# Single-block expert layers with the rows stationary, a start with the scores first, the last exponentials reordered, scatters spread

## The chip, the cores and the metric

The kernel runs on one core of a Trainium2 chip. The metric is the device time of one execution in microseconds. A run here gives the median of several executions. All executions in this document are of the fast state; the granted clock of TensorE is given where it matters. The four batches of runs were timed on whatever chip they got, and the kernel before stood in each at 783.5, 796.53, 783.53 and 784.12 us. So only kernels of one batch are compared directly, or each with the kernel before of its own batch.

## The reference

```python
# attention: q, k, v (8, 8, 576, 64), s (8, 8, 576), all float32
scores = scale * np.matmul(q, k.transpose(0, 1, 3, 2))
cum = np.cumsum(np.maximum(s, 0.0), axis=-1)
bias = -(cum[:, :, :, None] - cum[:, :, None, :])
scores = np.where(causal, -1000000000.0, scores + np.minimum(bias, 0.0))
attn = softmax(scores);  x = attn @ v               # then heads side by side: (8, 576, 512)
# experts: 8 of them, w1 (8, 512, 1024), w2 (8, 1024, 512)
fresh_e = argmax(x[b, s] @ w_gate)
e = fresh_e if s == 0 or local_gate[b, s] < 0.5 else prev_e
h = np.maximum(x[b, s] @ w1[e], 0.0)
out[b, s] = p[e] * (h @ w2[e])                      # p = softmax of the gate's logits
```

(Shortened: softmax written as a word, loops left out.)

## The kernel before

Attention goes through 32 pairs of heads. The rows that come out are scattered into one list per expert in DRAM. Then the experts run in units: a "double" has two blocks of 128 rows, a "single" has one, and a "mixed" unit has two half blocks of two experts. For a unit, rows are gathered, transposed by VectorE (`xT`), go through the first layer (`layer1`, into `hT`) and the second (`layer2`), and the output rows are scattered. In `mm`, `lhsT` is the stationary operand and `rhs` the moving one. The trace shows each float32 multiplication as two records. "Tail" in the names is the last 64 of the 576 positions.

The start: idle multiplications (`spin(n)`, n products of the identity with itself, there to bring TensorE's clock up), the biases, and then the loop over pairs.

```python
    spin(18)
    nc.vector.tensor_scalar_max(s_sb, s_sb, 0.0)
    cum = t_in.tile([BH, S], F32, name="cum")
    nc.vector.tensor_tensor_scan(cum, ones, s_sb, 0.0, op0=Alu.mult, op1=Alu.add)
    # ... cut: rel = cum - cum[mid] for two groups, 3 + 6 transposes into one bank (bps) ...
    nc.vector.tensor_copy(bias, bps[:, :at])
    # ... cut ...
    tail_scores(0)
    for n in range(NPAIR + 1):
        load(n + 3)
        if n < NPAIR:
            for u, pieces in enumerate((((0, 0), (3, 1)), ((0, 1), (1, 1)), ((2, 0), (2, 1), (1, 0)))):
                scores(n, u)
                for piece in pieces:
                    weights(n, piece)            # exponentials, ScalarE
        # ... cut ...
        if n:
            rows(n - 1, 1); divide(n - 1, 1); rows(n - 1, 0)     # products with v, division
        else:
            spin(8)
        if n + 1 < NPAIR:
            tail_scores(n + 1)
        if n:
            divide(n - 1, 0)
        if n < NPAIR:
            gate_parts(n); beside_v(n)           # VectorE's transpose into v
```

The first layer. With two weights (mixed units) the rows are the stationary operand, with one they are the moving operand, 128 columns for a single and 256 for a double:

```python
        if len(w) > 1:
            # ... cut ...
                for c in range(DK):
                    for h in range(2):
                        d = slice(h * HALF, h * HALF + HALF)
                        mm(ps[d], lhsT=xT[i][:, c, d], rhs=w[h][:, c, f], start=(c == 0), stop=(c == DK - 1))
                nc.scalar.activation(hx[i][:, f], ps, Act.Relu)
            if last == FK:
                x = hx.pop(i).rearrange("p (f n) -> p f n", f=FK)
                for a in range(0, P, m):
                    for d in range(0, P, m):
                        nc.vector.transpose(hT[i][d : d + m, :, a : a + m], x[a : a + m, :, d : d + m])
            return
        per = 512 // n
        for g in range(first, last, per):
            ps = ps_h.tile([P, 512], F32, name="hp")
            for j in range(per):
                f = (g + j) * P
                y = ps[:, j * n : j * n + n]
                for c in range(DK):
                    mm(y, lhsT=w[0][:, c, f : f + P], rhs=xT[i][:, c, :], start=(c == 0), stop=(c == DK - 1))
```

Of the kernel before, what the change touches and what calls it, by code (L numbers as in the profile page):

```python
# [10 lines left out]
F32 = mybir.dt.float32  # L11
I32 = mybir.dt.int32
Act = mybir.ActivationFunctionType
# [5 lines left out]
P = 128  # L19
# [51 lines left out]
def kernel(  # L71
# [33 lines left out]
    with ExitStack() as main:  # L105
# [47 lines left out]
        for j in range(8):  # L153
# [7 lines left out]
        check = in_range(main.enter_context(tc.tile_pool(name="g_sb", bufs=1)), nc, recs, sort.total, sort.ones, out_of)  # L161
        hooks = [(2, last.choose), (2, last.codes), (6, last.rows), (6, last.fresh), (6, last.held), (8, last.share),
                 (11, last.hold), (11, last.hot), (13, last.count), (13, last.rank), (15, last.gates),
                 (16, lambda bank: [f(bank) for f in last.scatters]),
                 *((18 + 2 * i, lambda bank: next(tables, None)) for i in range(8)),
                 *((60 + 6 * i, lambda bank, f=f: f(bank)) for i, f in enumerate(check))]
        experts(tc, w1, w2, out, rows_d, ident, sort, early_units() + units(), hooks, x4, gx, ready)
    def number(x, most):
        return nc.values_load(x[0:1, 0:1], min_val=0, max_val=most, skip_runtime_bounds_check_because="a count")
# [44 lines left out]
def attention(ctx, tc, q, kz, vz, vx, s, w_gate, w_local, ident, lg, recs, keep, new_x, plan):  # L214
# [75 lines left out]
        for i in range(n):  # L290
            mm(banks[1][:, :P], lhsT=ident, rhs=ident, start=True, stop=True)  # L291

    spin(18)
    nc.vector.tensor_scalar_max(s_sb, s_sb, 0.0)
    cum = t_in.tile([BH, S], F32, name="cum")
    nc.vector.tensor_tensor_scan(cum, ones, s_sb, 0.0, op0=Alu.mult, op1=Alu.add)


    bps = ps_s.tile([P, 2, 512], F32, name="bps", tag="s")[:, 0]
    bias_of, at = {}, 0  # L300
    for g, (q0, q1) in enumerate(GROUPS):
        n = -(-q1 // P) * P if g == 0 else S
        rel = t_in.tile([BH, n], F32, name=f"rel{g}")
        nc.vector.tensor_scalar(rel, cum[:, :n], cum[:, MIDS[g] : MIDS[g] + 1], None, Alu.subtract)
        for c, a in enumerate(range(0, TS, P)):
            if a + P <= n:
                tr(bps[:, at : at + BH], rel[:, a : a + P], ident[:BH, :BH])
                bias_of[c, g] = at
                at += BH
    tail_bias = at  # L310
    for h in range(2):
        mm(bps[h * TL : h * TL + TL, at : at + NPAIR], lhsT=rel[:, TS:], rhs=ident[:BH, h:BH:2], start=True, stop=True)
    at += NPAIR
    bias = once.tile([P, at], F32, name="bias")
    nc.vector.tensor_copy(bias, bps[:, :at])
    at = bias_of[2, 0]
    nc.vector.memset(bias[TL:, at : at + BH], MASKED)
    tmp.close()
    p_sc = pool("p_sc", 2, reuse_waits="tile")

    def scores(n, u):

        qb, kb = ins[n][:2]
        ps = raw[u] = ps_s.tile([P, 2, 512], F32, name="ps", tag="s")
        scs[n, u] = p_sc.tile([P, 2, sum(z - a for _, _, a, z in UNITS[u])], F32, name=f"sc{u}")
        runs = []
        for c, g, a, z in UNITS[u]:
            if runs and runs[-1][0] == c and runs[-1][2] == a:
                runs[-1][2] = z
            else:  # L330
                runs.append([c, a, z, PIECE[c, g][1]])
        for c, a, z, at in runs:
            for h in range(2):
                d = slice(DH * h, DH * h + DH)
                mm(ps[:, h, at : at + z - a], lhsT=kb[d, c * P : c * P + P], rhs=qb[d, a:z],  # L335
                   start=True, stop=True)

    def weights(n, *pieces):

        for c, g in pieces:  # L340
            u, at, a, z = PIECE[c, g]
            for h in range(2):
                i = bias_of[c, g] + 2 * n + h
                nc.scalar.activation(scs[n, u][:, h, at : at + z - a], raw[u][:, h, at : at + z - a], Act.Exp,  # L344
                                     bias=bias[:, i : i + 1], scale=scale)
            if min(c * P + P, S) <= z and (c, g) in PIECE:
                at += c * P - a
                if at >= 0:
                    x = scs[n, u][:, :, at : at + P]
                    nc.gpsimd.affine_select(out=x, in_=x, compare_op=Alu.is_ge, fill=0.0, base=0,  # L350
                                            pattern=[[0, 2], [1, P]], channel_multiplier=-1)

    def tail_scores(n):
        for h in range(2):
            d = slice(DH * h, DH * h + DH)
            mm(scores_of_tail[d], lhsT=ins[n][1][:, TS:][:, d], rhs=ins[n][0][:, TS:], start=True, stop=True)  # L356

    def tail(n):

# [71 lines left out]
        t = ps_s.tile([P, 2, 512], F32, name="bank", tag="s")  # L431
        return [t[:, i] for i in range(n)]

    tail_scores(0)
    for n in range(NPAIR + 1):
        load(n + 3)
        if n < NPAIR:
            for u, pieces in enumerate((((0, 0), (3, 1)), ((0, 1), (1, 1)), ((2, 0), (2, 1), (1, 0)))):
                scores(n, u)
                for piece in pieces:  # L440
                    weights(n, piece)
                    if piece == (0, 0):
                        tail(n)
                for f in plan.pop((n, 3 + u), ()):
                    f(bank)
            seen_tail(n)
        for f in plan.pop((n, 0), ()):
            f(bank)
        if n:
            rows(n - 1, 1)  # L450
            divide(n - 1, 1)
            rows(n - 1, 0)
# [8 lines that stand above are left out]
            gate_parts(n)  # L461
            beside_v(n)
        if n and n % HP == 0:
            logits(n // HP - 1)
        for half in (1, 2):
            for f in plan.pop((n, half), ()):
                f(bank)
# [653 lines left out]
def experts(ctx, tc, w1, w2, out, rows_d, ident, sort, units, hooks=(), w3=None, gx=None, ready=None):  # L1121
# [86 lines left out]
    def layer1(i, first, last):  # L1208
# [4 lines left out]
        if first == 0:  # L1213
            hT[i] = fp.tile([P, FK * 2 * P], F32, name="hT")[:, : FK * n].rearrange("p (f n) -> p f n", f=FK)
        w = [ws[s][:, : DK * F].rearrange("p (c f) -> p c f", c=DK) for s in of[i]]
        if len(w) > 1:

            if first == 0:
                hx[i] = w3[:, WS : WS + F] if ready else fp.tile([P, F], F32, name="hx", bufs=1)
            for g in range(first, last, FK // 2):  # L1220
                ps = ps_h.tile([P, 512], F32, name="hp")
                f = slice(g * P, g * P + 512)
                for c in range(DK):
                    for h in range(2):
                        d = slice(h * HALF, h * HALF + HALF)
                        mm(ps[d], lhsT=xT[i][:, c, d], rhs=w[h][:, c, f], start=(c == 0), stop=(c == DK - 1))
                    tick()
                nc.scalar.activation(hx[i][:, f], ps, Act.Relu)  # L1228
            if last == FK:
                x = hx.pop(i).rearrange("p (f n) -> p f n", f=FK)  # L1230
                m = P // 4
# [4 lines that stand above are left out]
# [46 lines left out]
    if ready:  # L1282
# [4 lines left out]

        layer1(1, 0, FK)
        load(0)
        fetch(2)  # L1290
        fetch(3)
        for k in range(2):
            layer2(0, k)
        load(1)
        for k in range(2):
            turn_x(2, k)
# [71 lines left out]
```

## Time and profile before

| | before |
|---|---|
| median, range | 783.39 us, 782.95 to 784.17 |
| span of the profiled execution | 782.4 us |
| TensorE / VectorE / ScalarE / GpSimd busy | 99 / 43 / 30 / 23 % |
| TensorE's waits of 0.3 us and more | 1.6 at the start, 0.8 and 0.3 at the end of attention |
| pair 1's first score | 14.39 us |
| first expert multiplication | 241.87 us |
| start of the last run of multiplications | 755.09 us |

TensorE is full, so a change pays if it takes work off TensorE or closes one of these few gaps. The last three rows cut the span into pieces that can be compared one by one: the start up to 14.39, attention from there to 241.87 (227.48 us), the experts to 755.09 (513.22 us), and the rest (27.3 us). The lines themselves stand in the prediction below.

### The profile page before, as it was taken

To read this page: it belongs to the slowest core of one execution; us is meant where nothing else is said; L and a number is where in the kernel's file an instruction comes from. 1 tells how busy PE (TensorE), PEld (TensorE's weight loads), DVE (VectorE), ACT (ScalarE), POOL (GpSimd) and SP (SyncE) were. 2 spreads that over 40 slices of the span, in tenths; PEclk is the share of its full clock that TensorE was granted. 3 is DMA by queue.
4 is the path that set the end of the run, shared out by engine and by line. 5 is a ranking of instruction groups with operands and counts; after the bars stand their busy time and mean duration, and the time that the engine had idled before them with its cause. 6 is when DMAs were issued, how large, how long until landed. Compare 5 with 4: busy or idle time off the path is not lost.

```text
span 782.4 us, 17629 instructions
## 1 busy us (share of the span) xinstructions
PE 773.0 (99%) x6782; PEld 546.2 (70%) x6782; DVE 339.0 (43%) x1196; ACT 237.2 (30%) x611; POOL 176.2 (23%) x329
## 2 busy tenths in 40 slices
PE   9999999999999999999999999999999999999996
PEld 8888888888887846836677366773657736676762
DVE  2334444455566748315562156521565215635000
ACT  5777767776762111111111111111111111111110
POOL 4432345456450421011110111101111011011001
PEclk9999999999999999999999999999999999999999
DMA  9586679988655499966997569976699766994001
GB/s 314 187 300 194 201 244 327 326 285 262 210 208 217 131 354 390 409 228 221 376 395 297 199 224 380 392 290 208 233 365 389 297 211 228 368 409 175 10 13 44
DMA packets 64141, 205.56 MB, mean 263 GB/s; under 512 B 8269, under 2 KB 8301, under 8 KB 64048
## 3 DMA queue, kind: packets, MB, share of 16 engines
q1 hardware_dynamic: 55008, 173.55, 62.3%
q0 software_dynamic: 8896, 30.47, 10.4%
q8 instruction: 55, 0.90, 0.5%
q10 hardware_dynamic: 144, 0.33, 0.1%
q14 instruction: 38, 0.31, 0.1%
HBM read 181.08 MB, written 23.76 MB: 262 GB/s over the span
## 4 chain that ended last, share of the span: by engine, by line
issue 58%; PE 32%; POOL 5%; DVE 2%; POOLq 2%; DMA 1%; DVEq 0%
PE o L406 14%; PE ps L335 11%; POOL out_dram L1261 2%; POOL xg L1196 2%; PE hp L1243 2%; PE o L374 2%; PE o L291 1%; POOLq L1171 1%; DMA x_rows<-x,r_slot_i 1%; PE o L356 1%; PE bank L956 0%; DVE xT L1097 0%; POOL x_rows L1047 0%; PE bank L1107 0%; PE bank L981 0%
## 5 line engine op out<-in xcount | busy, mean ns | idle before, releaser
L1097 DVE STREAM_TRANSPOSE xT<-xg 32x128 f32<-32x128 f32 x576 | 174.1, 302 | 174.2 <-PE hp L1243 92.7
L1256 PE MATMUL yp<-w,hT 128*128 128x512 f32 (+1 forms) x528 | 216.4, 593 | 0.0
L1243 PE MATMUL hp<-xT,w 128*128 128x256 f32 (+1 forms) x1088 | 192.3, 337 | 0.3 <-DVE xT L1097 0.3
L1243 PEld LDWEIGHTS hp<-xT,w 128*128 128x128 f32 x1088 | 172.1, 191 | 24.6 <-issue 8.2
L344 ACT ACTIVATE sc<-ps,bias 128x256 f32<-128x256 f32 (+3 forms) x448 | 156.5, 482 | 53.6 <-PE ps L335 51.2
L1256 PEld LDWEIGHTS yp<-w,hT 128*128 128x128 f32 (+1 forms) x528 | 90.1, 180 | 114.6 <-issue 113.3
L1261 POOL DMA_INDIRECT out_dram<-y,at_gate x38 | 38.5, 1013 | 433.9 <-ACT y L1260 419.0
L406 PE MATMUL o<-v,sc 128*64 128x74 f32 x3072 | 113.6, 228 | 0.8 <-issue 0.8
L406 PEld LDWEIGHTS o<-v,sc 128*64 128x64 f32 x3072 | 108.8, 136 | 8.1 <-issue 4.3
L1247 ACT ACTIVATE hT<-hp 128x512 f32<-128x512 f32 x68 | 40.6, 597 | 193.0 <-PE hp L1243 193.0
L1260 ACT ACTIVATE y<-yp,at_gate 128x512 f32<-128x512 f32 x38 | 26.1, 687 | 239.8 <-PE yp L1256 233.6
L335 PE MATMUL ps<-q,k 64*128 64x320 f32 (+2 forms) x768 | 92.5, 386 | 0.1
L350 POOL TENSOR_SCALAR_AFFINE_SELECT sc<-sc 128x256 f32<-128x256 f32 x160 | 66.5, 420 | 115.9 <-issue 59.1
L335 PEld LDWEIGHTS ps<-q,k 64*128 64x128 f32 x768 | 68.9, 186 | 20.0 <-issue 4.8
L1256 PE MATMUL yp<-x,hT 128*128 128x512 f32 (+1 forms) x144 | 63.2, 594 | 0.0
L1234 DVE STREAM_TRANSPOSE hT<-x 32x256 f32<-32x256 f32 x64 | 27.9, 436 | 65.4 <-ACT x L1228 64.5
L1243 PEld LDWEIGHTS hp<-xT,x 128*128 128x128 f32 x320 | 46.1, 191 | 5.8 <-issue 2.6
L1243 PE MATMUL hp<-xT,x 128*128 128x128 f32 (+1 forms) x320 | 50.1, 317 | 0.0
L416 DVE RECIPROCAL recs<-o 128x4 f32<-128x4 f32 x64 | 12.1, 189 | 87.0 <-PE o L406 63.1
L1256 PEld LDWEIGHTS yp<-x,hT 128*128 128x128 f32 (+1 forms) x144 | 25.3, 178 | 26.2 <-issue 26.0
L1047 POOL DMA_INDIRECT x_rows<-x,r_slot_i x40 | 38.7, 968 | 10.1 <-issue 5.9
L419 DVE TENSOR_TENSOR x<-o,recs 128x292 f32<-128x292 f32 x64 | 34.4, 538 | 2.2
(162 smaller groups left out, 339.8 us busy)
## 6 DMA issues: line engine op xcount, KB each, us to landing
w<-in_w_dram SPq DMA_DIRECT2D x184, 512.0 KB, 9.5
x<-in_w_dram SPq DMA_DIRECT2D x56, 512.0 KB, 9.3
v<-in_vx_dram SPq DMA_DIRECT2D x32, 405.0 KB, 5.8
vt<-in_vz_dram SPq DMA_DIRECT2D x32, 320.0 KB, 3.9
k<-in_kz_dram SPq DMA_DIRECT2D x31, 320.0 KB, 5.1
q<-in_q_dram SPq DMA_DIRECT2D x32, 288.0 KB, 5.4
xg<-x_rows POOLq DMA_DIRECT2D x30, 293.0 KB, 8.5
x_rows<-r_empty SPq DMA_DIRECT2D x6, 293.0 KB, 3.6
```

Source lines behind the costliest of these rows:

```text
L335: mm(ps[:, h, at : at + z - a], lhsT=kb[d, c * P : c * P + P], rhs=qb[d, a:z], start=True, stop=True)
L344: nc.scalar.activation(scs[n, u][:, h, at : at + z - a], raw[u][:, h, at : at + z - a], Act.Exp, bias=bias[:, i : i + 1], scale=scale)
L350: nc.gpsimd.affine_select(out=x, in_=x, compare_op=Alu.is_ge, fill=0.0, base=0, pattern=[[0, 2], [1, P]], channel_multiplier=-1)
L406: mm(y, lhsT=w, rhs=x, start=start, stop=stop)
L419: nc.vector.tensor_tensor(x, y, rec.unsqueeze(3).to_broadcast([P, t1 - t0, 2, HW]), op=Alu.mult)
L1047: self.s.nc.gpsimd.indirect_dma_start(out=next(self.s.views)[:, :], out_offset=bass.IndirectOffsetOnAxis(ap=self.slot[:z, m : m + 1], axis=0),
L1097: self.nc.vector.transpose(self.xT[i][d : d + m, :, k * P + a * m : k * P + a * m + m], rows[a * m : a * m + m, :, X0[d // DH] + d % DH :] ...
L1234: nc.vector.transpose(hT[i][d : d + m, :, a : a + m], x[a : a + m, :, d : d + m])
L1243: mm(y, lhsT=w[0][:, c, f : f + P], rhs=xT[i][:, c, :], start=(c == 0), stop=(c == DK - 1))
L1247: nc.scalar.activation(hT[i][:, g : g + per], ps, Act.Relu)
L1256: mm(ps[n * m : n * m + m, :], lhsT=hT[i][:, c, a : a + m], rhs=wn[:, c, :], start=(c == 0), stop=(c == FK - 1))
L1261: nc.gpsimd.indirect_dma_start(out=next(outs)[:, :], out_offset=bass.IndirectOffsetOnAxis(ap=at[i, k][:, 0:1], axis=0), in_=y[:, :], eleme ...
```

## The change

It has four parts. (1) A single's first layer takes the form of the mixed units: rows stationary, weights moving with 512 columns, and then 16 block transposes by VectorE. (2) At the start fewer idle multiplications; tail scores and first scores go before the biases, the two groups of biases are copied apart, and ScalarE makes the second group's difference. (3) The last pair's exponentials run in order of use. (4) The last ten scatters are spread over more places, and the gathers of units 2 and 3 go behind half of a second layer.

```diff
-                 (16, lambda bank: [f(bank) for f in last.scatters]),
+                 *((16 + 2 * i, f) for i, f in enumerate(last.scatters)),
@@ start
-    spin(18)
+    spin(8)
     ... (cum as before)
+    tail_scores(0)
+    scores(0, 0)
     ...
+        if g == 0:
+            nc.vector.tensor_scalar(rel, cum[:, :n], cum[:, MIDS[g] : MIDS[g] + 1], None, Alu.subtract)
+        else:
+            nc.scalar.activation(rel, cum, Act.Identity, bias=minus)
     ... (3 transposes of group 0, 6 of group 1, each into its own bank)
+        nc.vector.tensor_copy(bias[:, first : first + width[g]], bps[:, g, : width[g]])
+        if g == 0:
+            scores(0, 1)
@@ loop over pairs
-            for u, pieces in enumerate((((0, 0), (3, 1)), ((0, 1), (1, 1)), ((2, 0), (2, 1), (1, 0)))):
-                scores(n, u)
+            for u, pieces in enumerate((((0, 0), (3, 1)), ((0, 1), (1, 1)), ((2, 0), (2, 1), (1, 0)))
+                                       if n < NPAIR - 1 else
+                                       (((3, 1),), ((0, 1), (1, 1)), ((2, 0), (2, 1), (0, 0), (1, 0)))):
+                if n or u == 2:
+                    scores(n, u)
@@ layer1
-        if len(w) > 1:
+        if nbs[i] == 1:
     ...
+            m = P // len(w)
-                    for h in range(2):
-                        d = slice(h * HALF, h * HALF + HALF)
-                        mm(ps[d], lhsT=xT[i][:, c, d], rhs=w[h][:, c, f], start=(c == 0), stop=(c == DK - 1))
+                    for h, wh in enumerate(w):
+                        d = slice(h * m, h * m + m)
+                        mm(ps[d], lhsT=xT[i][:, c, d], rhs=wh[:, c, f], start=(c == 0), stop=(c == DK - 1))
@@ units 0 and 1
+        layer2(0, 0)
         fetch(2)
         fetch(3)
-        for k in range(2):
-            layer2(0, k)
+        layer2(0, 1)
```

(Cut: the moved definition of `tail_scores`, a second place for `hx`, tile allocation.)

More of the change, by code (lines that the diff above doesn't have):

```diff
@@ L163 @@
                  (11, last.hold), (11, last.hot), (13, last.count), (13, last.rank), (15, last.gates),
-                 (16, lambda bank: [f(bank) for f in last.scatters]),
+                 *((16 + 2 * i, f) for i, f in enumerate(last.scatters)),
                  *((18 + 2 * i, lambda bank: next(tables, None)) for i in range(8)),
                  *((60 + 6 * i, lambda bank, f=f: f(bank)) for i, f in enumerate(check))]
+        hooks.sort(key=lambda hook: hook[0])
         experts(tc, w1, w2, out, rows_d, ident, sort, early_units() + units(), hooks, x4, gx, ready)
@@ L291, in spin @@
             mm(banks[1][:, :P], lhsT=ident, rhs=ident, start=True, stop=True)
-    spin(18)
-    nc.vector.tensor_scalar_max(s_sb, s_sb, 0.0)
-    cum = t_in.tile([BH, S], F32, name="cum")
-    nc.vector.tensor_tensor_scan(cum, ones, s_sb, 0.0, op0=Alu.mult, op1=Alu.add)
-    bps = ps_s.tile([P, 2, 512], F32, name="bps", tag="s")[:, 0]
-    bias_of, at = {}, 0
-    for g, (q0, q1) in enumerate(GROUPS):
-        n = -(-q1 // P) * P if g == 0 else S
-        rel = t_in.tile([BH, n], F32, name=f"rel{g}")
-        nc.vector.tensor_scalar(rel, cum[:, :n], cum[:, MIDS[g] : MIDS[g] + 1], None, Alu.subtract)
-        for c, a in enumerate(range(0, TS, P)):
-            if a + P <= n:
-                tr(bps[:, at : at + BH], rel[:, a : a + P], ident[:BH, :BH])
-                bias_of[c, g] = at
-                at += BH
-    tail_bias = at
-    for h in range(2):
-        mm(bps[h * TL : h * TL + TL, at : at + NPAIR], lhsT=rel[:, TS:], rhs=ident[:BH, h:BH:2], start=True, stop=True)
-    at += NPAIR
-    bias = once.tile([P, at], F32, name="bias")
-    nc.vector.tensor_copy(bias, bps[:, :at])
-    at = bias_of[2, 0]
-    nc.vector.memset(bias[TL:, at : at + BH], MASKED)
-    tmp.close()
-    p_sc = pool("p_sc", 2, reuse_waits="tile")
     def scores(n, u):
@@ L324, in scores @@
         ps = raw[u] = ps_s.tile([P, 2, 512], F32, name="ps", tag="s")
-        scs[n, u] = p_sc.tile([P, 2, sum(z - a for _, _, a, z in UNITS[u])], F32, name=f"sc{u}")
         runs = []
@@ L336, in scores, with tail_scores @@
                    start=True, stop=True)
+    def tail_scores(n):
+        for h in range(2):
+            d = slice(DH * h, DH * h + DH)
+            mm(scores_of_tail[d], lhsT=ins[n][1][:, TS:][:, d], rhs=ins[n][0][:, TS:], start=True, stop=True)
+    spin(8)
+    nc.vector.tensor_scalar_max(s_sb, s_sb, 0.0)
+    cum = t_in.tile([BH, S], F32, name="cum")
+    nc.vector.tensor_tensor_scan(cum, ones, s_sb, 0.0, op0=Alu.mult, op1=Alu.add)
+    bps = ps_s.tile([P, 2, 512], F32, name="bps", tag="s")
+    tail_scores(0)
+    scores(0, 0)
+    bias_of, width = {}, [0, 0]
+    bias = once.tile([P, 7 * BH + NPAIR], F32, name="bias")
+    minus = t_in.tile([BH, 1], F32, name="minus")
+    nc.vector.tensor_scalar(minus, cum[:, MIDS[1] : MIDS[1] + 1], -1.0, None, Alu.mult)
+    for g, (q0, q1) in enumerate(GROUPS):
+        n = -(-q1 // P) * P if g == 0 else S
+        rel = t_in.tile([BH, n], F32, name=f"rel{g}")
+        if g == 0:
+            nc.vector.tensor_scalar(rel, cum[:, :n], cum[:, MIDS[g] : MIDS[g] + 1], None, Alu.subtract)
+        else:
+            nc.scalar.activation(rel, cum, Act.Identity, bias=minus)
+        first = width[0] * g
+        for c, a in enumerate(range(0, TS, P)):
+            if a + P <= n:
+                tr(bps[:, g, width[g] : width[g] + BH], rel[:, a : a + P], ident[:BH, :BH])
+                bias_of[c, g] = first + width[g]
+                width[g] += BH
+        if g == 1:
+            tail_bias = first + width[g]
+            for h in range(2):
+                mm(bps[h * TL : h * TL + TL, g, width[g] : width[g] + NPAIR], lhsT=rel[:, TS:],
+                   rhs=ident[:BH, h:BH:2], start=True, stop=True)
+            width[g] += NPAIR
+        nc.vector.tensor_copy(bias[:, first : first + width[g]], bps[:, g, : width[g]])
+        if g == 0:
+            at = bias_of[2, 0]
+            nc.vector.memset(bias[TL:, at : at + BH], MASKED)
+            scores(0, 1)
+    tmp.close()
+    p_sc = pool("p_sc", 2, reuse_waits="tile")
     def weights(n, *pieces):
@@ L341, in weights @@
             u, at, a, z = PIECE[c, g]
+            if (n, u) not in scs:
+                scs[n, u] = p_sc.tile([P, 2, sum(z - a for _, _, a, z in UNITS[u])], F32, name=f"sc{u}")
             for h in range(2):
@@ L351, in weights @@
                                             pattern=[[0, 2], [1, P]], channel_multiplier=-1)
-    def tail_scores(n):
-        for h in range(2):
-            d = slice(DH * h, DH * h + DH)
-            mm(scores_of_tail[d], lhsT=ins[n][1][:, TS:][:, d], rhs=ins[n][0][:, TS:], start=True, stop=True)
     def tail(n):
@@ L432, in bank @@
         return [t[:, i] for i in range(n)]
-    tail_scores(0)
     for n in range(NPAIR + 1):
@@ L437, in attention @@
         if n < NPAIR:
-            for u, pieces in enumerate((((0, 0), (3, 1)), ((0, 1), (1, 1)), ((2, 0), (2, 1), (1, 0)))):
-                scores(n, u)
+            for u, pieces in enumerate((((0, 0), (3, 1)), ((0, 1), (1, 1)), ((2, 0), (2, 1), (1, 0)))
[3 more added lines that the diff above has]
+                    scores(n, u)
                 for piece in pieces:
                     weights(n, piece)
-                    if piece == (0, 0):
+                    if piece == pieces[0] and u == 0:
                         tail(n)
@@ L1215, in layer1 @@
         w = [ws[s][:, : DK * F].rearrange("p (c f) -> p c f", c=DK) for s in of[i]]
-        if len(w) > 1:
+        if nbs[i] == 1:
             if first == 0:
-                hx[i] = w3[:, WS : WS + F] if ready else fp.tile([P, F], F32, name="hx", bufs=1)
+                at_ = WS + len(hT) % 2 * F
+                hx[i] = w3[:, at_ : at_ + F] if ready else fp.tile([P, F], F32, name="hx", bufs=1)
+            m = P // len(w)
             for g in range(first, last, FK // 2):
@@ L1223, in layer1 @@
                 for c in range(DK):
-                    for h in range(2):
-                        d = slice(h * HALF, h * HALF + HALF)
-                        mm(ps[d], lhsT=xT[i][:, c, d], rhs=w[h][:, c, f], start=(c == 0), stop=(c == DK - 1))
+                    for h, wh in enumerate(w):
+                        d = slice(h * m, h * m + m)
+                        mm(ps[d], lhsT=xT[i][:, c, d], rhs=wh[:, c, f], start=(c == 0), stop=(c == DK - 1))
                     tick()
```

## The prediction

> **What bounds the kernel now.** I read the page first (engines, chain, groups), then TensorE's timeline from start to end, then all engines in the three places that the change touches. Columns of the groups: count | busy us, mean ns | idle before. Of the timeline: start us, duration us, engine, line, instruction, count, idle before.
>
> ```profile
> PE 773.0 (99%) x6782; PEld 546.2 (70%) x6782; DVE 339.0 (43%) x1196; ACT 237.2 (30%) x611; POOL 176.2 (23%) x329
> L1234 DVE STREAM_TRANSPOSE hT<-x 32x256 f32<-32x256 f32 x64 | 27.9, 436 | 65.4 <-ACT x L1228 64.5
> ```
>
> TensorE (PE) is busy 99% of the span: only work taken off it, or its few gaps, can pay. Its waits add up to under 3 us: 1.6 at the very start, 0.8 and 0.3 where attention ends. VectorE (43%), ScalarE (30%) and GpSimd (23%) have room.
>
> The units with one block of rows ("singles"; ten of them run, I counted them in the timeline):
>
> ```profile
> 371.93 7.09 PE L1256 MATMUL yp<-w,hT 128*64 128x512 f32 x32
> 378.94 7.41 PE L1243 MATMUL hp<-xT,x 128*128 128x128 f32 x64
> 386.19 7.03 PE L1256 MATMUL yp<-w,hT 128*128 128x512 f32 x16
> 393.06 13.98 PE L1243 MATMUL hp<-xT,w 128*128 128x256 f32 x64
> ...
> 747.94 7.31 PE L1243 MATMUL hp<-xT,w 128*128 128x128 f32 x64
> 755.09 20.77 PE L1256 MATMUL yp<-w,hT 128*128 128x512 f32 x48
> ```
>
> A single's first layer is 32 matmuls, in the trace 64 records, of 128 columns: 747.94 to 755.09 is 7.15 us from start to start. Its second layer, the same multiplications with 512 columns each, is 16 records: 386.19 to 393.06 is 6.87 us. So one layer costs 0.28 us more than the other for the same arithmetic.
>
> The start:
>
> ```profile
> 1.55 7.06 PE L291 MATMUL o<-ident 128*128 128x128 f32 x36 [1.55 <-POOL ident masks.py:199]
> 6.57 0.84 DVE L304 TENSOR_SCALAR rel<-cum 64x384 f32<-64x384 f32 x2
> 8.55 0.65 PE L307 MATMUL bps<-ident,rel 64*128 64x64 f32 x7
> 9.36 0.34 PE L356 MATMUL o<-q,k 128*64 128x64 f32 x4
> 9.47 0.66 DVE L315 COPY bias<-bps 128x480 f32<-128x480 f32 x1 [2.07 <-PE bps L312]
> 9.62 2.86 PE L335 MATMUL ps<-q,k 64*128 64x320 f32 x24
> 10.86 0.95 ACT L344 ACTIVATE sc<-ps,bias 128x320 f32<-128x320 f32 x2 [7.98 <-PE ps L335]
> 12.41 2.05 PE L291 MATMUL o<-ident 128*128 128x128 f32 x16
> 14.39 0.34 PE L356 MATMUL o<-q,k 128*64 128x64 f32 x4
> ```
>
> Idle multiplications (L291) occupy TensorE until 8.55, then come bias transposes, scores of pair 0, more idle multiplications, and at 14.39 pair 1. From there pair follows pair every 6.79 us (scores at 15.07, 21.86, 28.66) with TensorE full. So 14.39 is the number that the start must beat.
>
> The end of attention:
>
> ```profile
> 237.56 0.34 DVE L377 STREAM_TRANSPOSE v<-o 128x160 f32<-128x160 f32 x1
> 237.94 3.78 DVE L1097 STREAM_TRANSPOSE xT<-xg 32x128 f32<-32x128 f32 x12
> 238.01 0.99 PE L406 MATMUL o<-v,sc 128*64 128x74 f32 x24 [0.83 <-issue]
> 241.87 5.42 PE L1243 MATMUL hp<-xT,w 128*128 128x256 f32 x24 [0.34 <-DVE xT L1097]
> ```
>
> The gap of 0.83 is labelled issue, but it ends 0.11 us after VectorE's transpose into v (end 237.90), which this product reads. The last exponentials ended at 236.66 and GpSimd's last mask at 237.14, both before. The 0.34 is for VectorE too (its transposes end at 241.72).
>
> **What the Trainium skill says.** "TensorE: Matmul & The Clock Gate", section "Back-to-back issue gap": N/2.4 + 2.5 ns warm, per matmul. "FP8 and Floating Point Precision", section "TensorE Precision Notes": true FP32 makes 4 passes. The trace agrees closely: two records to a matmul; a record starts 429.2 ns after the last at 512 columns (2 passes: 426.7 + 2.5) and 111.7 at 128 (106.7 + 5.0). Same page, Part 1 on the HAM clock gate: half clock until a window of about 3.4 us is busy, at a free-running phase, and gaps under that length keep the clock. The trace agrees: the idle multiplications start 213 ns apart until about 7.3 us, then 112. "ScalarE: Activation LUTs", section "Table sets: the hidden batching unit": cheap functions are in every set, so an Identity between exponentials should need no table load; the built program after the change indeed has one load, as before.
>
> **Part 1, singles with rows stationary.** Now 8 matmuls (16 records) of 512 columns in place of 64 records: 64 x 111.7 = 7.15 us becomes 16 x 429.2 = 6.87. That is 0.28 us on TensorE, ten times: **-2.8 us**. It lies wholly on the path. The half-array units between keep their switching cost (the first record of a run beside a unit with 64 rows starts some 0.09 late).
> The price: the result stands with rows on partitions, so VectorE gains 16 block transposes of 436 ns = 7.0 us per single (70 us in all, 43% to about 52%). In program order they stand before the next unit's row transposes. Tightest place, two singles and then a double: the first single's layer would end about 371.6, its values are ready at 372.3, VectorE runs to 379.5, then the double's 10.3 us of transposes (now 376.0 to 386.3, held by the rows' arrival) end at 389.8. The double begins about 392.5: 2.7 us to spare. The single's own second layer comes at least 13.7 us after its first. So nothing lands on the path.
>
> **Part 2, the start.** Idle multiplications fall from 18 to 8: 16 records x 213 = 3.4 us, to 4.97. Then TensorE waits for q of pair 0, whose completion stands in the trace at 6.02 (k at 4.05). From 6.1 it does tail and first scores, the first group's 3 transposes, second scores, the second group's 6, then third scores. These need the bank of the biases, so they wait for the second copy; then 8 idle multiplications, then pair 1. I take the work from the trace (warm): 0.27, 0.97, 0.24, 0.86, 0.57, copy with its hand-overs about 0.76, 0.96, 2.0. ScalarE makes the second group's difference (576 columns, about 0.7 us) between 6.7 and 7.5, off TensorE's path.
> If the clock is already full at 6.1, pair 1 begins at 12.7: 1.7 us earlier. If not, everything from 6.1 runs at half speed until a busy window has passed. With the gap of 1.1 us between, that is somewhere from 8.6 to 12: pair 1 begins between 14.0 and 15.6. The kernel before has the same lottery (full clock between 5 and 8.4: pair 1 from 13.4 to 15). I weigh warm 1 in 4, cold 3 in 4, and get **-0.1 us, give or take 0.7**. ScalarE starts at 8.4 to 9.9 instead of 10.86, but its lead is not what TensorE waits for: pair 1's scores need banks that are free in time either way.
>
> **Part 3, last pair's exponentials.** **0**: the gap before the last products is VectorE's, as shown.
>
> **Part 4, scatters spread, gathers later.** On GpSimd's own queue the ten scatters still stand in a row: **0**. Moving the gathers for units 2 and 3 behind half of a second layer puts one output scatter (1.04 us) before them: they were issued at 282.46, now at about 283.5. Their row transposes ended at 298.85, now about 299.9; unit 2 begins at 302.2. Hidden, 2.3 us to spare.
>
> Sum: 783.39 - 2.8 - 0.1 = 780.5; I add 0.2 for small waits that I can't see: **780.7 us**.
>
> **The rivals.** (a) The start pays: the full clock comes early, or the overlap carries further than I think, 1.5 us more: 779. For it: TensorE was held by idle multiplications although the differences were ready at 7.41. Against: the half clock. (b) The start costs: the late clock stretches scores and biases, +1: 781.8. For it: the gap at 5 to 6.1 is new. (c) VectorE becomes late: 7 us more before a double's rows. If the rows arrive 3 us later than here, each pair of singles loses up to a microsecond, four times, and eats part 1: 784. Against it: 2.7 us to spare. (d) Stationary rows save nothing, because the moving operand comes from the weights at another pace: 783.4. Against: the second layers have just this form and run at 429.2.
>
> **Range and chances.** Spread of the runs before: 1.2 us. Part 1 is sure to some 0.3, the start to 0.7; (c) has a tail upward. So 779.4 to 782.2 eight times in ten. Two per cent is 15.7 us, and nothing here is of that size: within 2% 0.985, faster 0.01, slower 0.005.
>
> **What would show it.** Single's first layers of 16 records, 6.87 us to the next; 64 + 160 of the L1234 kind on VectorE; no new idle time on TensorE before doubles; pair 1's scores near 15; the gap of 0.83 still there; units 2 and 3 on time. Wrong, if TensorE waits for row transposes after singles, if records with stationary rows start more than 430 ns apart, or if pair 1 begins before 13 or after 16.

## The result, and the profile after

The kernel after ran in 780.82 us (779.62 to 781.46, four executions), the kernel before beside it in 783.5. The ratio is 0.9964, with a 95% interval of 0.9946 to 0.9981: within 2%, and 0.1 us from the predicted 780.7. Ratios in this document are the mean time of one kernel's fast runs over that of the other's fast runs of the same rounds, so not quite the ratio of the medians.

The same cut of the span for the two profiled executions, each figure a difference of two starts in TensorE's timeline:

| piece | before | after | difference |
|---|---|---|---|
| start, to pair 1's first score | 14.39 | 14.56 | +0.17 |
| attention, to the first expert multiplication | 227.48 | 227.35 | -0.13 |
| experts, to the last run | 513.22 | 510.46 | -2.76 |
| the rest of the span | 27.3 | 27.4 | +0.1 |
| span | 782.4 | 779.8 | -2.6 |

Everything that the change gained in this pair of executions stands in the experts. The page of the kernel after, engines and the group of block transposes (count | busy us, mean ns | idle before):

```profile
PE 768.7 (99%) x6282; PEld 502.5 (64%) x6282; DVE 408.1 (52%) x1357; ACT 237.7 (30%) x612; POOL 174.6 (22%) x329
...
L1256 DVE STREAM_TRANSPOSE hT<-x 32x256 f32<-32x256 f32 x224 | 97.6, 436 | 133.1 <-ACT x L1250 130.1
```

VectorE rose from 43% to 52%: there are 224 block transposes in place of 64, as worked out (160 more), each still 436 ns. TensorE's records fell by 500. Its timeline where two singles meet a double, and at the last run:

```profile
378.74 7.13 PE L1248 MATMUL hp<-x,xT 128*128 128x512 f32 x16
385.71 7.03 PE L1278 MATMUL yp<-w,hT 128*128 128x512 f32 x16
392.57 13.98 PE L1265 MATMUL hp<-xT,w 128*128 128x256 f32 x64
...
745.50 7.03 PE L1248 MATMUL hp<-w,xT 128*128 128x512 f32 x16
752.37 20.76 PE L1278 MATMUL yp<-w,hT 128*128 128x512 f32 x48
```

The single's first layer now has 16 records, and no line carries an idle time. From 745.50 to 752.37 is 6.87 us, as predicted. From 378.74 to 385.71 is 6.97 us: 6.87, and 0.1 for the switch after a unit with half the array (`128*64`). Before, the layer at this place took 7.25 us (378.94 to 386.19). VectorE in the same place:

```profile
372.45 7.18 DVE L1256 STREAM_TRANSPOSE hT<-x 32x256 f32<-32x256 f32 x16 [8.19 <-ACT x L1250]
...
379.66 5.05 DVE L1116 STREAM_TRANSPOSE xT<-xg 32x128 f32<-32x128 f32 x16
384.86 5.04 DVE L1116 STREAM_TRANSPOSE xT<-xg 32x128 f32<-32x128 f32 x16
```

The single's own transposes come first, then the double's two blocks of rows, which end at 384.86 + 5.04 = 389.90. The double begins at 392.57, so 2.7 us are to spare.

TensorE's start in the kernel after:

```profile
1.55 3.78 PE L292 MATMUL o<-ident 128*128 128x128 f32 x16 [1.55 <-POOL ident masks.py:199]
6.29 0.48 PE L313 MATMUL o<-q,k 128*64 128x64 f32 x4 [0.95 <-DMA q<-in_q_dram]
6.70 2.08 PE L307 MATMUL ps<-q,k 64*128 64x320 f32 x8
...
11.51 1.13 PE L307 MATMUL ps<-q,k 64*128 64x320 f32 x8 [0.56 <-DVE bias L349]
12.58 2.05 PE L292 MATMUL o<-ident 128*128 128x128 f32 x16
14.56 0.34 PE L313 MATMUL o<-q,k 128*64 128x64 f32 x4
```

The idle multiplications end at 5.33, and q comes 0.95 us later. The eight first records of scores take 2.08 us, against 1.13 for the eight of the third scores: the first stand at half clock. The trace's record of the clock has full speed from 9.91 us here, from 7.41 before. The scores come three microseconds earlier than before and gain nothing.

The end of attention, TensorE:

```profile
238.14 0.99 PE L422 MATMUL o<-v,sc 128*64 128x74 f32 x24 [0.83 <-issue]
...
241.91 2.42 PE L1265 MATMUL hp<-xT,w 128*128 128x256 f32 x10 [0.25 <-DVE xT L1116]
```

The gap of 0.83 is the same to the hundredth. The start was 0.17 late, and here only 0.04 of that is left: the wait for VectorE's transposes shrank from 0.34 to 0.25. The gathers of units 2 and 3, from GpSimd's timeline:

```profile
282.85 1.00 POOL L1283 DMA_INDIRECT out_dram<-y,at_gate  x1 [7.82 <-ACT y L1282]
284.52 1.20 POOL L1215 DMA_DIRECT2D xg<-x_rows  x2 [0.68 <-DMA w<-in_w_dram]
```

They were issued at 282.46 before and at 284.52 now: 2.1 us later, not 1.0. The scatter in front of them starts 0.4 us after the old moment, as it waits for ScalarE's `y`, and takes 1.0; the gather then starts another 0.7 later, by its label for the load of `w`.

### The profile page after: what moved, and what is told of

It is laid out like the page before. It is cut to its first block, busy times and chain, and to the rows that moved or that the text cites. A ratio compares the mean times of both kernels' runs of the same rounds, so it can differ in the third digit from the quotient of the medians.

```text
span 779.8 us, 16796 instructions
## 1 busy us (share of the span) xinstructions
PE 768.7 (99%) x6282; PEld 502.5 (64%) x6282; DVE 408.1 (52%) x1357; ACT 237.7 (30%) x612; POOL 174.6 (22%) x329
## 4 chain that ended last, share of the span: by engine, by line
issue 58%; PE 31%; POOL 4%; DVE 3%; POOLq 2%; DMA 1%; SPq 0%; DVEq 0%
PE o L422 14%; PE ps L307 11%; POOL out_dram L1283 2%; POOL xg L1215 2%; PE hp L1265 2%; PE o L390 2%; POOLq L1190 1%; DMA w<-in_w_dram 1%; PE o L313 1%; DMA q<-in_q_dram 1%; PE bank L975 0%; DVE xT L1116 0%; SPq L1078 0%; PE bank L1126 0%; PE bank L1000 0%
## 5 line engine op out<-in xcount | busy, mean ns | idle before, releaser
L1256 DVE STREAM_TRANSPOSE hT<-x 32x256 f32<-32x256 f32 x224 | 97.6, 436 | 133.1 <-ACT x L1250 130.1
L1265 PE MATMUL hp<-xT,w 128*128 128x256 f32 x640 | 140.9, 380 | 0.2 <-DVE xT L1116 0.2
L1265 PEld LDWEIGHTS hp<-xT,w 128*128 128x128 f32 x640 | 121.1, 190 | 20.5 <-issue 4.2
L307 PE MATMUL ps<-q,k 64*128 64x320 f32 (+2 forms) x768 | 94.8, 391 | 0.8 <-DVE bias L349 0.6
L1248 PE MATMUL hp<-w,xT 128*128 128x512 f32 (+1 forms) x208 | 77.8, 595 | 0.0
L1269 ACT ACTIVATE hT<-hp 128x512 f32<-128x512 f32 x48 | 28.6, 597 | 134.4 <-PE hp L1265 134.4
L1248 PEld LDWEIGHTS hp<-w,xT 128*128 128x128 f32 (+1 forms) x208 | 29.8, 165 | 46.5 <-issue 46.5
L1250 ACT ACTIVATE x<-hp 128x512 f32<-128x512 f32 x28 | 16.7, 597 | 79.1 <-PE hp L1248 79.1
```

The lines of the kernel that those rows point to most:

```text
L307: mm(ps[:, h, at : at + z - a], lhsT=kb[d, c * P : c * P + P], rhs=qb[d, a:z], start=True, stop=True)
L1248: mm(ps[d], lhsT=xT[i][:, c, d], rhs=wh[:, c, f], start=(c == 0), stop=(c == DK - 1))
L1269: nc.scalar.activation(hT[i][:, g : g + per], ps, Act.Relu)
```

## The experiments

Twelve kernels ran, in three batches. "Control" is the kernel after once more.

### First batch: the parts alone (kernel before: 796.53 us)

This chip ran both kernels about 13 us slower than the first. The time went into the second half of attention and into a stall at 282 to 286 us: TensorE stood still twice, for 1.0 to 1.6 and for 1.0 to 1.75 us, labelled issue, in all four profiles, whatever part of the change was in. What holds the engines there I could not settle. The ratios are used, and no difference of the kernels is explained from that stall.

**Singles alone.** The kernel before with this edit:

```diff
-        if len(w) > 1:
+        if nbs[i] == 1:
             (rows stationary for one weight too, as in the change)
```

> Only part 1 of the change (a single's first layer with its rows stationary), the start, the last pair and the scatters as before. My theory: the gain of the change is this part. Ten first layers of 7.15 us become 6.87: 2.7 to 2.8 us off, so about 780.7 with 783.5 for the kernel before; from the first expert matmul to the last run of second layers about 510.5 us instead of 513.2. Rival A (the start brings the gain, VectorE's extra transposes eat part of the singles'): 782 or more, and TensorE waits before doubles.

Measured: 793.48 us (792.75 to 793.77), ratio 0.996 (0.9946 to 0.9973). 0.4% of 796.53 is 3.2 us; by the interval it is 2.2 to 4.3. From the first expert multiplication to the last run its profile has 515.34 us, not 510.5: the stall and a window at half clock behind it lie in this stretch. The profile of the start alone, whose singles are as before, has both too and takes 517.97. That is 2.63 us more, and TensorE nowhere waits for rows after singles, so rival A falls.

**Start alone.**

```diff
-    spin(18)
+    spin(8)
+    tail_scores(0)
+    scores(0, 0)
     (biases apart, second difference on ScalarE, as in the change)
```

> Only part 2 (the start). My theory: nothing on the mean, within 0.7 us of before, but a lottery of TensorE's clock: pair 1's first matmul (14.4 before) between 12.7, where the clock is full by 6 us, and 15.6, where it becomes full at 12; in the profile it follows the moment of the full clock. Rival A: it gains 1 to 2.7 us in every run, as ScalarE's first exponential comes 1.3 us sooner. Rival B: it always costs 0.2 or more, as pair 1 came 0.17 later in the one profile.

Measured: 795.99 us (795.52 to 797.92), ratio 1.0001 (0.9985 to 1.0017). The start neither pays nor costs in this batch, within 1.3 us. In its profile the clock was full at 7.55 us and pair 1 began at 12.97. Of rival A only the lowest edge (1 to 1.2 us) is left; rival B's 0.2 us is less than these runs resolve.

**Last exponentials, scatters and gathers alone.**

```diff
-                 (16, lambda bank: [f(bank) for f in last.scatters]),
+                 *((16 + 2 * i, f) for i, f in enumerate(last.scatters)),
+                                       (((3, 1),), ((0, 1), (1, 1)), ((2, 0), (2, 1), (0, 0), (1, 0)))
+        layer2(0, 0)
         fetch(2)
```

> Only parts 3 and 4 (last pair's exponentials in order of use, scatters spread, gathers for units 2 and 3 later). My theory: 0, within 0.3 us of before: the gap of 0.83 us before the last pair's products stands, as VectorE's transpose ends it; gathers are issued 1 us later and unit 2 still begins on time. Rival A: the gap shrinks and 0.5 to 0.8 us are gained. Rival B: unit 2 waits for its rows, a loss of up to 1 us.

Measured: 796.32 us (795.28 to 798.11), ratio 1.0003 (0.9989 to 1.0018): nothing within 1.4 us. The gap of 0.83 stands in its profile too, so rival A falls, and unit 2 does not wait, so rival B falls. But the slack is nearly used up. On this chip unit 2's rows were ready at 312.69 and unit 2 began at 313.42, 0.7 us later; in the profile of the start alone, with the gathers where they were, they were ready 8.8 us ahead.

**The whole change again.** No edit.

> The changed kernel once more, unchanged, for the spread between executions and for a second profile of it. My theory: runs from 779.5 to 781.5, 2.7 us under before on the mean, and those runs early in which the clock was full early. If the sum of the three parts alone (singles -2.75, start 0, end 0) differs from this by over 0.7 us, the parts act on each other and the theory is incomplete.

Measured: 793.31 us (791.43 to 794.83), ratio 0.9954 (0.9937 to 0.997). The product of the three parts, 0.996 x 1.0001 x 1.0003 = 0.9964, lies inside this interval. By the ratios the whole gains 0.8 us more than the product of its parts, by the medians 0.6 us less than their sum: the limit of 0.7 us that I had set is finer than these runs resolve. The only part with a gain clear of noise is the singles'.

### Second batch: what the start could have paid (kernel before: 783.53 us)

**Control.**

> The kernel after the change once more, as a control for the three runs beside it, which all start from it. Theory (the singles pay 2.8 us, the new start pays nothing because TensorE idles for q of pair 0 and so is moved about by its clock): 0.995 to 0.998 of the kernel before on whatever chip this is, and pair 1's tail scores at 13.4 to 14.9 us in the profile, with the full clock from somewhere between 5.5 and 10 us. Rival (the start does pay, and the first call just did not resolve it): 0.993 or less.

Measured: 779.76 us (779.4 to 784.47, six executions, one far above the rest), ratio 0.9964 (0.9945 to 0.9983). TensorE's start in its profile:

```profile
5.51 0.34 PE L313 MATMUL o<-q,k 128*64 128x64 f32 x4 [0.31 <-DMA q<-in_q_dram]
...
12.63 0.34 PE L313 MATMUL o<-q,k 128*64 128x64 f32 x4
```

Same program, other luck: q came 0.8 us earlier, and the clock was full at 4.92 us. Pair 1 starts at 12.63 instead of 14.56, which was below the 13.4 that I had expected. It is near the warm case of the prediction (12.7), in part by luck: the first scores began at 5.51, 0.6 earlier than the sum had them, and from there to pair 1 it was 7.1 us instead of 6.6, 0.3 of them a wait for the differences. The pieces behind are those of the first profile: 227.37 us of attention and 510.46 of experts.

**More idle multiplications first.**

```diff
-    spin(8)
+    spin(11)
```

> After, with 11 idle multiplications in the first run of them instead of 8, so that TensorE is busy, if with nothing, until q of pair 0 lands. Theory (the idle gap of about 1 us before the first scores is what delays the full clock and eats the gain of the start): the full clock comes between 5 and 8.4 us at whatever phase, pair 1's tail scores start at 12.9 to 14.0 us, and the kernel is 0.4 to 1.2 us faster than its control. Rival (the start is bound by something else, ScalarE's exponentials or the copy of the biases, and the clock only shifts idle time about): pair 1 starts at the same 13.4 to 14.9 us and the time is within 0.3 us of the control. The spread of the runs is about 1 us, so the place of pair 1 in the profile counts for more than the median.

Measured: 780.46 us (779.96 to 780.86), ratio 0.9957 (0.9944 to 0.997). The clock was full at 5.37 us and pair 1 began at 13.74, in the range expected. But in this execution the first scores began only at 7.17, 1.1 us after the idle multiplications ended, so the edit does not close the wait when q is late (the label names an instruction of VectorE that these scores do not read; the trace's semaphore events, which `prof` does not list, have the last of q's 16 landings at 7.03, 0.14 us ahead of the scores, and in all eleven profiles of the new start this distance is 0.13 or 0.14). The mean of the five executions, 780.41, is 0.3 us under the control's 780.68, which has the outlier in it; the medians have it the other way round. So no gain in time is shown. The five executions lie within 0.9 us, the control's six within 5.

**No idle multiplications behind the third scores.**

```diff
-        else:
-            spin(8)
```

> After, without the 8 idle multiplications behind the third scores (2.0 us of them at full clock). Theory (those multiplications stand on TensorE's path to pair 1, whose first steps need nothing else): pair 1's tail scores come right after pair 0's third scores, 1.5 to 2 us earlier, at 11.4 to 13 us; the first products of pair 0 then wait for its exponentials, so that of the 2 us some 0.5 to 1.5 remain in the time. Rival (ScalarE's exponentials of pair 0 set the start: they begin after the copy of the biases and take some 5 us): pair 1's scores come earlier, but pair 1's products come when they did, within 0.3 us, with the gap in TensorE before them, and the time is within 0.3 us of the control; it may even be slower if the gap costs the clock.

Measured: 778.46 us (778.22 to 780.25), ratio 0.9938 (0.9926 to 0.9951), the fastest kernel of all. TensorE in its profile, pair 1's first scores and pair 0's first products:

```profile
11.12 0.34 PE L313 MATMUL o<-q,k 128*64 128x64 f32 x4 [0.40 <-DMA k<-in_kz_dram]
...
14.83 0.99 PE L422 MATMUL o<-v,sc 128*64 128x74 f32 x24
```

The control has these at 12.63 and 16.10. The scores come 1.5 us earlier, the products 1.3, and the median fell by 1.3. Experts begin at 238.79 against 240.00. The rival falls: ScalarE does not set this place. The 0.4 is a new wait, for pair 1's k; it and small waits inside pair 1's scores keep back 0.7 of the 2.0 us of work taken out. Whether the kernel before would gain as much from this edit was not tried.

**Both.**

```diff
-    spin(8)
+    spin(11)
...
-        else:
-            spin(8)
```

> After with both edits: 11 idle multiplications first and none behind the third scores. If both theories hold the gains add, 1.0 to 2.5 us faster than the control, and this is the version that beats both kernels: about 0.993 of the kernel before. If ScalarE sets the start, then pair 0's first products stand where they stood, and the time is that of the control within 0.5 us.

Measured: 778.95 us (778.74 to 779.33), ratio 0.9939 (0.9926 to 0.9952). The gains do not add, since the first edit has none in the median. Pair 1 starts at 11.39, again behind its k. Against the kernel before, both this kernel and the last are clearly faster. Against the kernel after, the intervals of the ratios still overlap (0.9945 to 0.9952); for it speak the medians, 0.8 and 1.3 us lower, the starts in the traces, and that the slowest of these five executions, 779.33, lies under the fastest of the control, 779.4.

### Third batch: slack and order (kernel before: 784.12 us)

**Five block transposes more per full single.**

```diff
-                        nc.vector.transpose(hT[i][...], x[...])
+                        for _ in range(2 if len(w) == 1 and a + d < m * 2 + 1 and a * d == 0 else 1):
+                            nc.vector.transpose(hT[i][...], x[...])
```

> After, with 5 of a full single's 16 block transposes done twice: 5 x 0.436 = 2.2 us more of VectorE for each of the ten, into the same values. Theory (VectorE's rows for the double behind two singles are ready 2.6 us before they are needed): nothing reaches TensorE, the stretch from the first expert multiplication to the start of the last run stays at 510.5 us within 0.2 (on a chip that does not stall elsewhere), and no wait of TensorE for xT before a double. Rival (VectorE is already the bound or the slack is not what I read): some 0.5 to 2 us before each of the four doubles behind two singles, 2 to 8 us in all.

Measured: 780.72 us (779.44 to 782.23), ratio 0.996 (0.9944 to 0.9977). From the first expert multiplication to the last run it is 510.46 us, to the hundredth the kernel after. 22 us more of work on VectorE cost nothing.

**All sixteen twice.**

```diff
+                        for _ in range(1 + (len(w) == 1)):
+                            nc.vector.transpose(hT[i][...], x[...])
```

> After, with all 16 block transposes of a full single done twice: 7.0 us more of VectorE for each of the ten. Theory (2.6 us of slack, then every further microsecond shows): the double behind the first two singles starts 7.0 - 2.6 = 4.4 us late with TensorE waiting for xT, VectorE then works through without a break and the next double is late by some 4 us more; four such places with two doubles each, the last one shorter: 26 to 34 us more, about 1.033 of the kernel before. Rival (VectorE has the room of the page's 52% and the transposes are spread over it): under 3 us more.

Measured: 819.18 us (818.01 to 822.76), ratio 1.0453 (1.0423 to 1.0484). VectorE and TensorE at the double of before:

```profile
390.69 5.04 DVE L1116 STREAM_TRANSPOSE xT<-xg 32x128 f32<-32x128 f32 x16
...
395.83 14.05 PE L1266 MATMUL hp<-xT,w 128*128 128x256 f32 x64 [3.18 <-issue]
```

The rows are ready at 395.73, the double starts 0.1 us later, and the wait is labelled issue, like the 0.83 of attention: the label names no engine, and the moment does. The theory holds, and its sum was short: the experts took 548.79, so 38.3 us more, against 26 to 34 expected. TensorE's waits in this stretch add up to 27.2 us (19.1 before doubles, 6.9 for `hT` of singles, 1.2); one more of 1.8 lies behind it, in the last run. Five windows of 3.41 us stood at half clock after such waits; by their busy shares they cost 7.9 us. That is 35.1 of the 38.3; the rest is not accounted for. The half clock is the term that I had left out.

**Gathers early again.**

```diff
-        layer2(0, 0)
         fetch(2)
         fetch(3)
+        layer2(0, 0)
         layer2(0, 1)
```

> After, with the gathers of units 2 and 3 back in front of the first second layer, as they were before. Theory (the change put one output scatter in front of them; that ate slack and nothing else): their row transposes on VectorE end 1.0 to 2.6 us earlier than in a profile of the kernel after on the same chip, unit 2 begins at the same moment within 0.15 us of its unit 1, and the time is that of the kernel after within its spread (ratio to before 0.995 to 0.998). Rival (the late gathers cost part of the gain): the stretch from the first expert multiplication to the last run is shorter than 510.5 by 0.3 us or more and the ratio is under 0.995.

Measured: 780.47 us (779.7 to 781.26), ratio 0.995 (0.9934 to 0.9967), and a **wrong result** (NaN), which I had not meant. GpSimd's timeline says why this order can't stand:

```profile
282.34 1.13 POOL L1215 DMA_DIRECT2D xg<-x_rows  x2 [0.38 <-issue]
...
292.88 1.01 POOL L1066 DMA_INDIRECT x_rows<-x,r_slot_i  x1 [9.41 <-DMA xg<-x_rows]
```

With the scatters spread, the tenth stands behind the gathers in GpSimd's order; rows are read from DRAM before they are written. (That these are the rows with NaN is inferred from the order, not traced.) So the later gathers are no separate idea of the change: they are what spread scatters need. As for time, the multiplications are the same in number and size; the experts take 510.46 us again, so the late gathers cost nothing on this chip. Counted from the first expert multiplication, unit 2's row transposes end at 56.28 us, 3.4 earlier than the 59.68 of the run with five transposes more (1.0 to 2.6 were expected), and unit 2 begins at 60.32 in both: only slack was eaten.

**The transpose into v earlier.** For the last pair:

```diff
+        if n == NPAIR - 1:
+            gate_parts(n)
+            beside_v(n)
         if n:
             rows(n - 1, 1)
...
-        if n < NPAIR:
+        if n < NPAIR - 1:
```

> After, with the last pair's gate products and VectorE's transpose into v issued before the products of the pair ahead of it. Theory (the gap of 0.83 us at the end of attention is a wait for that transpose, which stands behind a division on VectorE; and VectorE also sets the moment at which the experts can begin): the gap of 0.83 before the last products shrinks to under 0.3, the wait for xT before the first expert multiplication grows from 0.25 by about as much, and the experts begin at the same distance from pair 30's scores within 0.2 us; the time is that of the kernel after. Rival 1 (the gap is ScalarE's exponentials or a mask): the gap stays over 0.6. Rival 2 (the gap is a loss in its own right): it goes, the experts begin 0.5 us or more earlier.

Measured: 783.95 us (782.14 to 788.61), ratio 1.001 (0.9972 to 1.0048), so some 3 us slower than its neighbours by the medians, 3.8 by the stretch below. VectorE and TensorE:

```profile
233.92 0.34 DVE L393 STREAM_TRANSPOSE v<-o 128x160 f32<-128x160 f32 x1
...
234.32 1.41 PE L422 MATMUL o<-v,sc 128*64 128x74 f32 x24 [1.94 <-DVE v L393]
```

The gap is indeed a wait for v, now by its label, which speaks against exponentials and masks as its cause in this order. But it grew to 1.94 instead of shrinking under 0.3: in VectorE's order v now stands behind the twelve row transposes (`xT`) that are issued with the pair ahead (229.96 to 233.75). The wait pulled the clock down for one window (234.74 to 238.15), and the wait for `xT` before the experts grew to 1.4. From the last pair's scores (the expectation names the wrong pair) to the first expert multiplication it is 15.15 us, against 11.36 in the kernel after. My expectation fell on each of its numbers. What stays of it is the cause of the gap; that it can't be had for nothing was right for a reason that I had not seen.

## Why the prediction was right

- **Part 1, singles.** -2.8 us predicted, -2.76 measured in the experts' stretch, and 0.996 for the singles alone. Sixteen records per single, 6.87 us to the next where no half-array unit stands before, VectorE at 52%: all as worked out. The rivals about VectorE and about stationary rows (784 and 783.4) fall.
- **VectorE's slack.** 2.7 us predicted, 2.7 read (the expectations have 2.6), and then tried: 2.2 us more of work cost nothing, 7.5 us more (32 block transposes took 14.72 us, the 16 of the kernel after 7.18) cost 5.0 at the first such double (it starts 155.63 us after the first expert multiplication, 395.83 less 240.20, and 150.66 in the kernel after).
- **Part 2, the start.** -0.1 predicted, +0.17 in the first profile, ratio 1.0001 alone. The work from the first scores to pair 1 was summed rightly: 6.6 us at full clock, and 6.57, 6.57 and 6.69 in the three profiles of this start in which neither the clock nor the differences hold it. The step that was mis-sized is "warm 1 in 4, cold 3 in 4". In eight profiles with exactly this start, full clock came between 4.82 and 6.04 us in five, at 7.55 in one, and at 9.85 and 9.91 in two. A second lottery was left out: q, put at 6.02, landed anywhere from 5.27 to 6.80 in these eight, so that pair 1 begins at 12.63 to 13.51 in the five warm ones (12.7 predicted) and at 14.40 and 14.56 in the two cold ones (14.0 to 15.6 predicted). Three began before 13, which the prediction names as a sign of being wrong, though its own warm case is 12.7. Pair 1 began at 13.41 on average in the eight, 0.9 below the 14.3 of the sum, and at 13.90 in the three profiles that have the start of before (14.39, 13.13, 14.19), 0.5 below the one trace that the sum was measured against. Both of its figures were too high, and most of the error cancels in the difference; that is luck. With so few profiles a gain of 0.5 us is possible, and not shown; the timed runs of the start alone don't resolve it.
- **The path through the start.** The prediction counted the eight idle multiplications behind the third scores as 2.0 us and asked only whether the start of before would be beaten. Taking them out gives 1.3 us, more than the whole of part 2.
- **Part 3, last exponentials.** 0 predicted, 0 measured (in one run with part 4), and the gap of 0.83 still there.
- **Part 4, scatters and gathers.** 0 in time, as predicted. The step that failed is "one output scatter (1.04 us) before them": that scatter also waits for ScalarE's `y`, until 282.85, and the gather behind it for 0.7 us more. So the gathers are issued 2.1 us later, the row transposes end at 301.38 instead of 298.75 (the prediction misread this as 298.85), 2.6 us later, and 0.85 us are to spare instead of 2.3. And "still stand in a row" missed why the gathers moved at all.
- **The clock rule.** "Gaps under that length keep the clock" was wrong. (Its "same page" is "TensorE: Matmul & The Clock Gate"; the clause was concluded from the page's idle window and not measured.) A gap of 1.94 us, four of six gaps of 3.18 us, and in three of the four slow profiles the two stalls of 1.0 to 1.75 us were followed by windows at half clock. It did no harm to the number, as nothing in the kernel after waits so long on the first chip once attention runs.

## What to carry to other kernels

On a full engine, count what one record costs from start to start in each form of the same multiplication, and price the work that the better form gives to another engine by the tightest place, not by its share of the span. Filler that keeps the clock up is on the path like any other work: ask for each piece of it whether the engine would really stand still without it. When one instruction is moved behind another on a queue, add what that other one waits for, and look for data that only the queue's order protects.

## What the Trainium skill lacked or had wrong

- "TensorE: Matmul & The Clock Gate", Part 1, the table of the two states, has the half clock return after an idle window of about 3.4 us, and the section on HAM oscillation speaks of idle gaps over that length. (Its section on a second failure mode tells of oscillation from short idles between groups of multiplications, without a measure.) Here windows of 3.41 us that were partly busy were followed by half clock: I laid windows of 3413 ns from the first full clock on, onto which every later change of the clock falls, and took the share of each in which multiplications run in the trace, over all fourteen profiles. At shares from 0.08 to 0.35, and once at 0.43, half clock followed; from 0.45 up full clock stayed, and at the end of three executions also at 0.42. A waiting engine needs no gap as long as the window, by these shares only some 57% of one.
- The same table asks for one busy window before full clock, without a measure. Here half-clock windows with a share up to 0.80 stayed at half clock (0.72 in both the kernel before and after), and from 0.85 up (0.85, 0.89, 0.90 and more) full clock followed. The free-running phase that the page states agrees: the first full clock lay anywhere from 4.65 to 9.91 us.
- The same page, "Back-to-back issue gap", calls N/2.4 + 2.5 ns isolated and gives about 81 ns (128 columns) and 131 ns (512) for a sustained stream, without the number format. The sustained FP32 stream here is at 111.7 ns and 429.2 ns per record of two passes, so 55.9 and 214.6 ns per pass: near the formula, and not at the sustained figures. (Part 1 of the page has 55.6 and 215.7 ns back to back, which is as near.) In the formula's terms the 128-column record pays the 2.5 ns twice, the 512-column record once. The doubles' record of 256 columns, at 216 ns, pays about once too, so the change's form would take about 0.1 us off a double's first layer (64 x 216 against 32 x 429.2, an estimate), against 0.28 off a single's.
- No page that I read says how far the same kernel can differ from one chip to the next: the kernel before had medians of 783.5, 796.53, 783.53 and 784.12 us in four batches. The record has the last three on three chips; whether chip or hour made the difference was not tried.
